# Other transfers of the wk words, products ahead of the first TensorE work, another order of the first tasks, and branch hints

## The chip, the cores and the metric

One NeuronCore of a Trainium2 chip runs the kernel. The metric is the device time of one execution in microseconds, the median of several runs. TensorE (PE; PEld is its weight load), VectorE (DVE), ScalarE (ACT), GpSimd (POOL) and SyncE (SP, which issues the DMAs here) each work through a list of their own and wait for each other by semaphores.

## The reference

Gated linear attention over 768 steps for 4 x 8 heads of width 48, then a channel mix over 3072 rows of 384:

```python
f = 1.0 / (1.0 + np.exp(-f_logit))
for t in range(S):
    state = f[:, :, t, :, None] * state + np.einsum('bhd,bhe->bhde', k[:, :, t], v[:, :, t])
    y[:, :, t] = np.einsum('bhd,bhde->bhe', q[:, :, t], state)
...
xk = mu_k * x + (1.0 - mu_k) * x_prev
xr = mu_r * x + (1.0 - mu_r) * x_prev
k = np.maximum(xk @ w_k, 0.0)
v = k * k @ w_v
r = 1.0 / (1.0 + np.exp(-(xr @ w_r)))
return (r * v).astype(np.float32)
```

## The kernel before

The attention runs in 24 chunks of 128 steps (index i), the mix in 8 units of 384 rows (index u); three chunks fill one unit. Everything is written as small named tasks, and the table ORDER sets, token by token, in which order the tasks' instructions stand; each engine gets its own instructions in that order. A suffix such as `:V` picks the engine where a task has several. HOMES names the buffer of each pool that a task takes.

The tasks of a chunk, in the order in which they depend on each other: loads `f`, `qk`, `v`; `sf` (DVE, a clamp of the logits); for the first six chunks `zT` (PE transposes), `ez` and `ln` (ACT), `b` (PE, running sums by a triangular matrix), `rb` and `e` (ACT); `q` (DVE) and `kr` (DVE or POOL) scale q and k; `TR` (PE transposes) and `kt` (copy) turn k; `SP` (PE, scores and state sums); `m` (mask), `zb` and `T` (DVE, the new state), `za` (POOL); `YA`, then `w`, then `YB` (PE, the chunk's output), `y` (ACT, the output into x and a stage). Then `sp` (16-row DMAs that spread the stage over x), `d`, `xm`, `xh`, `xl` (the mixed input, split in a high and a low part).

The tasks of a unit: `F` (8 groups of 9 products with wk), `r`, `h`, `kk`, `l` (the squares, split), `R` (3 groups of 9 with wr), `lg` and `sg` (the sigmoid), `W` (6 groups of 12 with wv), `o` and `out`. F0.0 is the first of these groups.

The weights arrive as 8-byte words. A piece p of wk, wr or wv passes `S`, `T`, `X` (DVE), `H` (ACT or DVE, the high part) and `L` (POOL or DVE, the low part). F0.f waits for wkL of its own 128 columns. wk comes in eight transfers of 384 KB, each with 128 of its 1024 columns, so that one row of a transfer is 1 KB; four land before the first unit and four later.

At the end, `lo` (DVE) reduces two checks to a column, `lot` (PE) transposes it, `lom` (DVE) makes a flag of it, and `strong` loads the flag into a register of every engine. After the token `?` stands a branch: where the flag is set, a slow general form runs in place of what was computed. With these inputs it is skipped. Only o7.2 and its transfer stand behind it.

`+n` puts n products of constants on PE (`fill`), which nobody reads.

Of the kernel before, what the change touches and what calls it, by code (L numbers as in the profile page):

```python
# [60 lines left out]
e4 wrH2 y1 qk5 wvX0 wrS3 wk1 wrT3 zb2 TR3 bl4 YA2 wrX3 m2 kr4 w2:V q4 q3 T2 kt3 wrH3 b5 wkL0 rb5 YB2 wrL3 v4 y2 wvS2 wkS3
sp0.0 TR4 SP3 wvT2 wvH0 wkT3 x00 za3:G wrL2 e5 sp0.2 wvL0 wvX2 zb3 YA3 wvH2 m3 sp0.1 kr5 wkS1 w3 kt4 v5 wrH0 YB3 y3 T3 za4:G
wvL2 d0.00 wkT1 SP4 q5 wk5 wkX1 wkX3 xm0.00 wr1 bl5 wkH1 d0.10 zb4 +2 YA4 d0.02 xh0.00 m4 wk4 TR5 w4 T4 wrL0 YB4 d0.01 xm0.02
wkL1 wk6 kt5 xl0.00 xm0.01 za5:G SP5 xm0.10 wk7 xh0.02 wv3 y4 zb5 x01 xh0.01 f2 wv4 m5 xl0.02 YA5 d0.12 d0.11 xl0.01 w5:V wkH3
xm0.12 YB5 wrS1 xh0.10 wkL3 F0.0 xm0.11 xl0.10 F0.1 xh0.11 y5 wrT1 xh0.12 wkS4 wrX1 wkS5 r0.0 wkT4 xl0.11 kk0.0:A wrH1 wkT5
xl0.12 wkX4 r0.1 F0.2 wkX5 wrL1 h0.0 kk0.1:A wkS6 wkT6 l0.0 R0.0 wkH5 wkS7 wkH4 r0.2 wkX6 wkL4 h0.1 wkH6 wkT7 F0.3 wkL6 l0.1:V
kk0.2:A wkX7 wvS3 F0.4 wkH7 wkL5 lg0.0 wvT3 wkL7 h0.2 r0.3 wvX3 kk0.3:A F0.5 l0.2 sp1.1 wvS4 wvH3 r0.4 h0.3 wvL3:V h0.4:G F0.6
kk0.4:A wvT4 wv5 r0.5 f3 l0.3:V wvX4 h0.5 sp1.0 l0.4:V F0.7 r0.6 kk0.6:A R0.1 kk0.5 qk7 sp1.2 r0.7 l0.5:V wvH4:V h0.7:G
kk0.7:A wvS5 qk8 R0.2 lg0.1 wvT5 wvX5 h0.6 qk6 l0.7 l0.6 W0.00 v7 wvL4:V lg0.2 wvH5 sg0 wvL5:V d1.0 W0.01 xm1.00 d1.1 xh1.00:V
xm1.11 W0.10 xm1.01 xl1.00:V sf3 xh1.01:V d1.2 W0.11 xm1.12 sf2 xl1.01 xm1.02 xm1.10 b6 xh1.02 ln6 xl1.02 W0.20 o0.0 o0.1  # L70
W0.21 out0.0 rb6 bl6 b7 c1 ln7 q7 q6 F1.0 rb7 kr6 xh1.10 bl7 kr7 o0.2 n7 v6 n6 out0.2 k7 F1.1 xl1.10 r1.0 v8 b8 kk1.0:A qk9
h1.0 l1.0 F1.2 r1.1 k6 ln8 kk1.1 rb8 TR6 q8 kr8 TR7 kt6 SP6 r1.2:V kt7 xh1.12 kk1.2 bl8:V b9 g8 h1.2 F1.3 zb6:A l1.2 xh1.11 n8
# [951 lines left out]
```

## Time and profile before

| | us |
|---|---|
| median of 3 runs | 337.22 (335.83 to 338.24) |
| the profiled execution, device time | 335.34 |
| its span, first to last instruction | 333.5 |
| PE busy in the span | 318.3 (95%) |
| DVE busy | 257.6 (77%) |

The profile is of one execution. The time is 1.8 us more than the span. [...] In a timeline row, the bracket is the engine's idle time before the instruction and what ended it. A row in which several instructions are merged has its count behind an x.

### The profile page before, as it was taken

How to read it: one execution, taken by the hardware profiler on the slowest of the kernel's cores; microseconds unless marked ns; L12 is line 12 of the kernel's file. 1: busy time of each engine (PE TensorE's matmuls, PEld its weight loads, DVE VectorE, ACT ScalarE, POOL GpSimd, SP SyncE). 2: the span in 40 equal slices, each digit the busy share in tenths (PEclk: the TensorE clock that was granted, in tenths of full speed). 3: DMA queues.
4: the chain of work that ended last, by engine and by line, in shares of the span. 5: the costliest groups of instructions: out<-in, count | busy, mean ns of one | idle time of the engine just before them, and what ended most of it. 6: DMA issues, size and time to landing. Idle time of an engine off the chain costs nothing.

```text
span 333.5 us, 10954 instructions
## 1 busy us (share of the span) xinstructions
PE 318.3 (95%) x4560; PEld 304.5 (91%) x4560; DVE 257.6 (77%) x517; ACT 180.9 (54%) x366; POOL 163.3 (49%) x212
## 2 busy tenths in 40 slices
PE   4896899999999999999999999999999999999994
PEld 4685789999999989999999998999999999999994
DVE  4898899999989988897877776698679817767530
ACT  3795888869376565593549234475247132604510
POOL 2278786377653434114762858317565015326500
PEclk9999699999999999999999999999999999999999
DMA  7987693834436333943315522506024003243001
GB/s 260 366 327 233 175 329 87 317 111 137 175 99 191 108 108 117 303 161 101 105 32 211 210 89 79 183 0 191 11 63 135 28 6 96 93 134 110 2 28 56
DMA packets 21370, 46.41 MB, mean 139 GB/s; under 512 B 3008, under 2 KB 13760, under 8 KB 21312
## 3 DMA queue, kind: packets, MB, share of 16 engines
q1 hardware_dynamic: 21312, 45.63, 41.4%
q8 instruction: 38, 0.62, 0.7%
q14 instruction: 20, 0.16, 0.1%
HBM read 38.54 MB, written 4.72 MB: 130 GB/s over the span
## 4 chain that ended last, share of the span: by engine, by line
PE 87%; DMA 5%; DVE 2%; ACT 2%; SPq 2%; issue 1%; POOL 0%; DVEq 0%; ACTq 0%
PE pm L561 72%; PE py L408 7%; PE pss L371 3%; DMA f<-in_zt 3%; PE pss L391 2%; DMA words_k2l<-in_wk 2%; PE py L349 2%; SPq L693 1%; PE pm L342 1%; POOL wv L707 0%; SPq L457 0%; ACT f L261 0%; PE py L766 0%; DVE qk L287 0%; SPq L232 0%
## 5 line engine op out<-in xcount | busy, mean ns | idle before, releaser
L561 PE MATMUL pm<-xh,wk 128*128 128x384 f32 x384 | 103.8, 341 | 0.9 <-DVE qk L295 0.6
L561 PEld LDWEIGHTS pm<-xh,wk 128*128 128x128 f32 x384 | 69.9, 187 | 2.1 <-DVE qk L295 1.1
L561 PE MATMUL pm<-xl,wk 128*128 128x384 f32 x192 | 64.7, 337 | 0.0
L584 ACT ACTIVATE r<-pm 128x384 f32<-128x384 f32 x46 | 22.4, 492 | 50.1 <-PE pm L561 43.7
L561 PE MATMUL pm<-wv,k2h 128*128 128x384 f32 x192 | 49.2, 338 | 0.0
L553 POOL TENSOR_TENSOR xl<-xm,xh 128x384 fp32r<-128x384 f32 x28 | 29.4, 1058 | 31.0 <-DVE xh L547 19.3
L601 POOL TENSOR_TENSOR k2l<-kk,k2h 128x384 fp32r<-128x384 f32 x32 | 34.1, 1069 | 17.7 <-ACT k2h L589 9.9
L287 POOL TENSOR_TENSOR qk<-qk,rb 128x256 f32<-128x256 f32 x21 | 16.0, 761 | 46.6 <-ACT bl L276 21.8
L561 PE MATMUL pm<-wr,xh 128*128 128x384 f32 x144 | 37.0, 338 | 0.0
L561 PEld LDWEIGHTS pm<-xl,wk 128*128 128x128 f32 x192 | 36.0, 188 | 0.4 <-issue 0.4
L590 POOL TENSOR_TENSOR k2h<-r 128x384 fp32r<-128x384 f32 x27 | 25.8, 958 | 21.2 <-ACT r L584 13.5
L561 PEld LDWEIGHTS pm<-wv,k2h 128*128 128x128 f32 x192 | 34.5, 188 | 0.2
L561 PE MATMUL pm<-wv2h,k2h 128*128 128x384 f32 x96 | 32.7, 341 | 0.0
L561 PE MATMUL pm<-wv2l,k2h 128*128 128x384 f32 x96 | 32.3, 336 | 0.0
L561 PE MATMUL pm<-wv,k2l 128*128 128x384 f32 x96 | 32.3, 336 | 0.0
L561 PE MATMUL pm<-wv2h,k2l 128*128 128x384 f32 x96 | 32.3, 336 | 0.0
L601 DVE TENSOR_TENSOR k2l<-kk,k2h 128x384 fp32r<-128x384 f32 x32 | 22.5, 707 | 8.7 <-ACT k2h L589 4.9
L561 PEld LDWEIGHTS pm<-wr,xh 128*128 128x128 f32 x144 | 25.8, 188 | 0.2
L408 PE MATMUL py<-qk,z 64*64 64x64 f32 x704 | 22.2, 233 | 3.7 <-DVE z L328 2.9
L538 DVE SCALAR_TENSOR_TENSOR xm<-pm,mu_sb,x 128x384 f32<-128x384 f32 x42 | 24.9, 610 | 0.8 <-POOL xl L553 0.5
L561 PE MATMUL pm<-wr,xl 128*128 128x384 f32 x72 | 24.2, 336 | 0.0
L595 POOL TENSOR_TENSOR kk<-r 128x384 f32<-128x384 f32 x14 | 12.5, 891 | 22.1 <-ACT r L584 14.6
(143 smaller groups left out, 702.4 us busy)
## 6 DMA issues: line engine op xcount, KB each, us to landing
qk<-in_qkt SPq DMA_DIRECT2D x24, 512.0 KB, 4.8
words<-in_wv SPq DMA_DIRECT2D x12, 512.0 KB, 4.6
f<-in_zt SPq DMA_DIRECT2D x7, 768.0 KB, 7.3
v<-in_vt SPq DMA_DIRECT2D x24, 192.0 KB, 3.9
out<-o SPq DMA_DIRECT2D x21, 192.0 KB, 2.1
...
```

Source lines behind the costliest of these rows:

```text
L287: e.tensor_tensor(k()[:, ::2], k()[:, ::2], rb()[:, ::2], op=ALU.mult)
L349: nc.tensor.transpose(self.py[:, r, 256 + 64 * j : 320 + 64 * j], k()[HALF[r], j], self.ident[HALF[r], HALF[r]])
L371: nc.tensor.matmul(self.pss[HALF[h], r, 64 * j : 64 * j + 64], k()[HALF[r], j, HALF[h]], q()[HALF[r], j, HALF[h ^ j % 2]], start=True, sto ...
L391: nc.tensor.matmul(self.pss[64 * r : 64 * r + D, h, n : n + D], self.b("ktk", i)[HALF[h], j, r], self.b("v", i)[HALF[h], 2 * j + r], start ...
L408: first[c, h] = nc.tensor.matmul(to, lhs, rhs, start=(c, h) not in first, stop=stop, skip_group_check=True)
L538: pl.add(f"xm{u}.{n}{j}", pr, ("V", 0.62, 0, lambda xm=xm, n=n, j=j: nc.vector.scalar_tensor_tensor(xm(), pm("d", u, j)[:, :UT], self.mu_s ...
L553: e.tensor_tensor(lo(), xm(), hi().bitcast(F32), op=ALU.subtract)
L561: nc.tensor.matmul(ps, lhs(a, j), rhs(bb, j), start=ends[0] and i == 0, stop=ends[1] and i == len(pr) - 1)
L584: pl.add(f"r{u}.{f}", kf, ("A", 0.5, 0, lambda r=r, ps=ps: nc.scalar.activation(r(), ps(), AF.Relu)), ("V", 0.56, 0, lambda r=r, ps=ps: nc ...
L590: ("G", 1.02, 0, lambda r=r, hi=hi: nc.gpsimd.tensor_tensor(hi(), r(), r(), op=ALU.mult)),
L595: ("G", 1.02, 0, lambda r=r, kk=kk: nc.gpsimd.tensor_tensor(kk(), r(), r(), op=ALU.mult)),
L601: e.tensor_tensor(lo(), kk(), hi().bitcast(F32), op=ALU.subtract)
```

## The change

Four things change.

- wk comes in four transfers of 768 KB. Three of them hold 768 columns of one third of wk's rows each (one row of a transfer is 6 KB), the fourth the last 256 columns. One such transfer makes two pieces. F0.0 to F0.2 now each wait for the three pieces wkL0, wkL1 and wkL2, F0.3 to F0.5 for wkL3, wkL4 and wkL5.
- Seven products of a new constant tile `warm` stand at the head of PE's list, and the later fills use the same tile. `warm` is set by DVE's first instruction.
- ORDER and HOMES are new. On PE the tasks of the attention's first six chunks are reordered, with fills of 7, 3, 2, 2 and 4 products where there were 3, 2 and 2; behind F0.0 few PE tasks change places, one of them `lot`.
- A branch hint stands ahead of the load of the flag on every engine, for the branch over the general form.

The diff, cut to its core. Of the two tables one line each stands here:

```diff
-f0.0 qk0 sf0.0 f0.2 cst mu zT0 f0.1 ez0 sf0.2 sf0.1 wr2 v0 wk2 ln0 qk1 wk0 +3 b0 f1 v1 wv1 rb0 zT1 kr0:V ez1 v2 e0 zT2 TR0 qk2
++7 f0.0 cst qk0 v0 v1 f0.1 mu f0.2 wr2 sf0.0 zT0 ez0 qk1 wk2 f1 ln0 +3 b0 sf0.1 rb0 zT1 wk0 wv1 qk2 kr0:V wrS2 ez1 qk3 ln1 v2
...
-    "words": "010101010010100110010",
+    "words": "010100101100101010101",
...
-                   + ([] if alone else [f"wkL{f}"]),
+                   + ([] if alone else [f"wkL{p}" for p in (range(f // KJ * KJ, f // KJ * KJ + KJ) if f < 2 * KJ else (f,))]),
...
+                for h in range(2):
+                    p = (6 if last else i) + (h if last else KJ * h)
...
+                    piece("wk", p, home, view, lambda i=i, last=last: self.wk[:, :, 6 * P :] if last else self.wk[:, i, : 6 * P],
...
+                          i, h == 0, whole, 6 * P)
...
     def fill(self, what):
 
         for _ in range(int(what)):
-            self.nc.tensor.matmul(self.py[:, 0, 256:384], self.low[:, 0], self.low[:, 1], start=False, stop=True,
-                                  skip_group_check=True)
+            to = self.tiles["pm"][3][:, :P] if self.cold else self.py[:, 0, 256:384]
+            self.nc.tensor.matmul(to, self.warm, self.warm, start=self.cold, stop=True, skip_group_check=True)
+        self.cold = False
...
         def load():
+            self.tc.mark_branch_hint_location("rest", "LikelyTaken", engines=mybir.ALL_ENGINES)
             self.strong = nc.values_load(self.flag, min_val=0, max_val=1)
...
+    nc.vector.memset(k.warm, LOW)
...
-    with tc.If(k.strong > 0):
+    with tc.If(k.strong > 0, label="rest"):
```

What the new tables do at three places follows; the numbers behind names are those of buffers.

PE's list at its head, before: `ident,f` is zT, `low` a fill, `tri,f` is b, `ident,qk` is TR, and the rows with pss are SP.

```order
L256 MATMUL pm_93<-ident,f_61 128x128 x4
L766 MATMUL py<-low 128x128 x3
L250 MATMUL pm_94<-tri,f_61 128x128 x4
L256 MATMUL pm_95<-ident,f_61 128x128 x4
L256 MATMUL pm_96<-ident,f_61 128x128 x4
L342 MATMUL pm_93<-ident,qk_64 128x128 x4
L250 MATMUL pm_95<-tri,f_61 128x128 x4
L371 MATMUL pss<-qk_64 64x64 x16
```

And now:

```order
L786 MATMUL pm_97<-warm 128x128 x7
L258 MATMUL pm_97<-ident,f_61 128x128 x4
L786 MATMUL py<-warm 128x128 x3
L252 MATMUL pm_95<-tri,f_61 128x128 x4
L258 MATMUL pm_96<-ident,f_61 128x128 x4
L786 MATMUL py<-warm 128x128 x2
L344 MATMUL pm_97<-ident,qk_64 128x128 x4
L252 MATMUL pm_96<-tri,f_61 128x128 x4
L373 MATMUL pss<-qk_64 64x64 x16
```

Seven products stand ahead of zT0, zT2 has gone from before TR0 to behind SP0, and a fill of two stands ahead of TR0.

DVE's list where the first piece of a late wk transfer is turned, before: L685, L696 and L699 are S, T and X of a piece, L328 is zb3, L383 m3, L334 T3.

```order
L279 TENSOR_TENSOR qk_67<-qk_67,pm_96 128x512
L334 TENSOR_TENSOR sm<-pss,z_75 128x192
L685 TENSOR_SCALAR pm_93<-words_122 128x512
L685 TENSOR_SCALAR pm_96<-words_k2l_132 128x384
L696 SCALAR_TENSOR_TENSOR pm_93<-words_122,pm_93 128x512
L696 SCALAR_TENSOR_TENSOR pm_96<-words_k2l_132,pm_96 128x384
L699 SCALAR_TENSOR_TENSOR words_122<-words_122,pm_93 128x512
L328 TENSOR_TENSOR z_77<-pss,z_76 128x4x48
L383 TENSOR_TENSOR ss_100<-pss,mask 128x512
```

And now (L385 is m3, L330 zb3, L336 T3):

```order
L687 TENSOR_SCALAR pm_95<-words_123 128x512
L385 TENSOR_TENSOR ss_101<-pss,mask 128x512
L699 SCALAR_TENSOR_TENSOR pm_95<-words_123,pm_95 128x512
L330 TENSOR_TENSOR z_78<-pss,z_77 128x4x48
L702 SCALAR_TENSOR_TENSOR words_123<-words_123,pm_95 128x512
L336 TENSOR_TENSOR sm<-pss,z_78 128x192
L687 TENSOR_SCALAR pm_97<-words_k2l_133 128x384
L699 SCALAR_TENSOR_TENSOR pm_97<-words_k2l_133,pm_97 128x384
L702 SCALAR_TENSOR_TENSOR words_k2l_133<-words_k2l_133,pm_97 128x384
```

The first instruction that needs the late wk transfer stood ahead of zb3 and now stands behind it, and behind T3.

PE's list at the end, before, from `lot` (L800) on; 20 more products of W7.10 and W7.11 follow the four below, then `TENSOR_LOAD flag`, then W7.20:

```order
L561 MATMUL pm_94<-wv2h,k2l_958 128x384
L800 MATMUL pm_93<-ident,xm_112 1x128 x2
L561 MATMUL pm_96<-wv_87,k2h_859 128x384
L561 MATMUL pm_96<-wv_88,k2h_859 128x384
L561 MATMUL pm_96<-wv_87,k2l_864 128x384
L561 MATMUL pm_96<-wv_87,k2h_859 128x384
```

And now, `lot` being L820, up to the first products of W7.20:

```order
L563 MATMUL pm_96<-wv2l,k2h_967 128x384
L563 MATMUL pm_96<-wv2h,k2l_970 128x384
L820 MATMUL pm_97<-ident,xm_112 1x128 x2
L1043 BRANCH_PREFETCH_HINT
L832 TENSOR_LOAD flag
L563 MATMUL pm_94<-wv_88,k2h_860 128x384
L563 MATMUL pm_94<-wv_89,k2h_860 128x384
```

Between `lot` and PE's load of the flag stood 24 products; now there is none.

## Rows read from the trace of the kernel before

**Rows 1.** The page's parts 1 and 2: busy time, and slices.

```profile
PE 318.3 (95%) x4560; PEld 304.5 (91%) x4560; DVE 257.6 (77%) x517; ACT 180.9 (54%) x366; POOL 163.3 (49%) x212
...
PEclk9999699999999999999999999999999999999999
```

**Rows 2.** Chain that ended last, in time: start, us, what.

```profile
33.59 1.56 PE py L408 x48
...
39.14 0.84 PE py L408 x48
...
45.06 33.27 PE pm L561 x189
...
320.59 8.39 PE pm L561 x48
```

**Rows 3.** Busy time by stretch: us, PE, PEld, DVE, ACT, POOL, clock, DMA share, GB/s.

```profile
30.00:36.40 6.40, 4.25 (x184) 3.97 (x176) 5.78 (x13) 2.85 (x10) 4.86 (x6) 0.64 0.37 110
36.40:41.71 5.31, 4.67 (x149) 3.85 (x140) 4.35 (x9) 5.10 (x14) 4.25 (x7) 0.79 0.78 232
```

**Rows 4.** DVE's timeline: start, us, engine, line, operation.

```profile
0.88 0.06 DVE L882 MEMSET sure<- 128x1 f32 x1 [0.88 <-PEq L1010]
...
3.62 0.49 DVE L460 TENSOR_SCALAR f<-f,sure 128x512 f32<-128x512 f32 x1 [0.33 <-DMA f<-in_zt]
...
9.10 0.43 DVE L287 TENSOR_TENSOR qk<-qk,rb 128x256 f32<-128x256 f32 x1 [2.10 <-ACT rb L263]
...
29.99 0.56 DVE L685 TENSOR_SCALAR pm<-words_k2l 128x384 int32<-128x384 int32 x1 [1.10 <-DMA words_k2l<-in_wk]
...
36.40 0.62 DVE L533 SCALAR_TENSOR_TENSOR xm<-x,one_mu,pm 128x384 f32<-128x384 f32 x1 [0.62 <-ACT pm L530]
```

**Rows 5.** PE's timeline up to the first product of F0.0.

```profile
4.25 1.09 PE L256 MATMUL pm<-ident,f 128*128 128x128 f32 x4 [4.25 <-DVE f L460]
5.13 1.49 PE L766 MATMUL py<-low 128*128 128x128 f32 x6
6.69 1.74 PE L250 MATMUL pm<-tri,f 128*128 128x128 f32 x8
...
10.63 1.16 PE L250 MATMUL pm<-tri,f 128*128 128x128 f32 x8 [0.17 <-ACT f L261]
...
32.62 0.71 PE L408 MATMUL py<-qk,z 64*64 64x64 f32 x16 [1.88 <-DVE z L328]
...
42.91 0.44 PE L561 MATMUL pm<-xh,wk 128*128 128x384 f32 x1
```

**Rows 6.** POOL's timeline: the last low parts ahead of F0.0.

```profile
40.15 2.05 POOL L553 TENSOR_TENSOR xl<-xm,xh 128x384 fp32r<-128x384 f32 x2 [0.17 <-ACT xh L546]
```

**Rows 7.** DMA issues by line: KB each, median us to landing.

```profile
f<-in_zt SPq DMA_DIRECT2D x7, 768.0 KB, 7.3
...
words_k2h<-in_wk SPq DMA_DIRECT2D x2, 384.0 KB, 7.6
```

**Rows 8.** The flag's tile, its makers and loads (duration min/median/max ns, start us).

```profile
L807 DVE SCALAR_TENSOR_TENSOR flag<-xm x1: 148/148/148, 321.2 to 321.2; 1x1 int32<-1x1 f32 x1
...
L811 PEldq TENSOR_LOAD <-flag x1: 487/487/487, 321.5 to 321.5; - x1
```

**Rows 9.** All engines' timeline from `lot` to o7.2.

```profile
320.21 0.38 PE L800 MATMUL pm<-ident,xm 128*1 128x128 f32 x2
320.32 0.30 PEld L561 LDWEIGHTS pm<-wv,k2h 128*128 128x128 f32 x2
...
329.06 0.56 DVE L655 TENSOR_TENSOR lg<-pm,lg 128x384 f32<-128x384 f32 x1 [3.68 <-PE pm L561]
```

**Rows 10.** Line 899, the branch: each engine's compare, and what follows it.

```profile
L899 SPq EVENT_SEMAPHORE  x8: 17/17/17, 328.4 to 329.0; - x8
...
L899 SPq COMPARE_BRANCH  x1: 45/45/45, 325.8 to 325.8; - x1
L899 DVEq EVENT_SEMAPHORE  x1: 21/21/21, 327.7 to 327.7; - x1
```

More of the change, by code (lines that the diff above doesn't have):

```diff
@@ L61 @@
[L61 to L72, printed above, removed]
@@ new lines @@
+wvH0 onemu wrL0 wrX3 ln5 wvS2 qk5 wrH3 b5 m3 wvT2 kt4 sp0.0 wkL3 wrL3 zb3 +2 YA3 rb5 wvL0 wvX2 sp0.1 T3 e5 w3 YB3 wvH2 SP4
+wkS1 za4:G v5 wkT1 d0.02 wkX1 y3 wvL2 xm0.02 q5 wkH1 wr1 kr5 bl4 zb4 wv4 d0.00 bl5 xm0.00 d0.01 wk3 +4 YA4 wkL1 TR5 m4 wv3 w4
+f2 xh0.00 T4 d0.10 xm0.01 xl0.00 YB4 xm0.10 qk6 kt5 xh0.02 SP5 za5:G y4 wrS1 xl0.02 xh0.01 zb5 d0.11 m5 xl0.01 YA5 wrT1 w5 YB5
+d0.12 xm0.11 xh0.10 wrX1 xl0.10 xh0.11 F0.0 wkS4 y5 xm0.12 wrH1 xl0.11 xh0.12 sp1.0 wkT4 wkS5 wkX4 F0.1 r0.0 sp1.1 wrL1 h0.0
@@ new lines @@
+W6.20 xm7.12 xm7.11 xh7.10 o6.1 W6.21 xh7.11 xh7.01:V cm12 out6.1 xl7.01:V F7.0 o6.2 cm2 c13 F7.1 F7.2 r7.0:V kk7.0:G xl7.10
+r7.1:V c10 h7.0 out6.2 F7.3 h7.1 l7.0 cm13 r7.2 kk7.1:A kk7.2 h7.2 r7.3:V l7.1 xh7.12 F7.4 h7.3:G kk7.3 xl7.11:V xl7.12 F7.5
+cm10 R7.0 r7.5:V F7.6 l7.2 r7.4 lg7.0:V kk7.4 l7.3:V h7.4 l7.4 r7.6:V kk7.5:A h7.5:G h7.6:G lo F7.7 r7.7:V h7.7:G R7.1 W7.00
+l7.5:V kk7.6 lg7.1 R7.2 l7.6 kk7.7:G l7.7 lg7.2:V W7.01 W7.10 W7.11 sg7 lot lom strong o7.0 out6.0 o7.1 out7.1 W7.20 W7.21
@@ L667, in add_words, with piece @@
         nc = self.nc
-        def piece(name, p, home, view, load, shape, hi, lo, first):
+        def piece(name, p, home, view, load, shape, hi, lo, src, first=True, whole=None, total=0, begins=True):
             place = WORDS[name][0] + WORDS[name][1] * p
@@ L690, in piece @@
             kept = [home] if home else []
-            tu = {"takes" if first else "uses": kept}
-            free = [f"wkL{j}" for j in range(4, 8)] if name == "wv" and p >= 3 and not clamp else []
-            pl.add(f"{name}{p}", place - 0.4, ("Q", n * P * 8 / 370e3, 1, lambda: nc.sync.dma_start(view(), load())), **tu)
+            free = [f"wkL{j}" for j in (2, 5, 6, 7)] if name == "wv" and p >= 3 and not clamp else []
+            if first:
+                pl.add(f"{name}{src}", place - 0.4, ("Q", (total or n) * P * 8 / 370e3, 1, lambda: nc.sync.dma_start(
+                    (whole or view)(), load())), **{"takes" if begins else "uses": kept})
             dve = us(0.00104, 0.15)
-            pl.add(f"{name}S{p}", place, ("V", dve, 0, shift), after=[f"{name}{p}"], takes=[t_key], uses=kept)
+            pl.add(f"{name}S{p}", place, ("V", dve, 0, shift), after=[f"{name}{src}"], takes=[t_key], uses=kept)
             pl.add(f"{name}T{p}", place, ("V", dve, 0, lambda: nc.vector.scalar_tensor_tensor(
@@ L847, in rwkv_kernel @@
     k.tri = cp.tile([P, P], F32, name="tri")
+    k.warm = cp.tile([P, P], F32, name="warm")
     k.sure = cp.tile([P, 1], F32, name="sure")
```

148 lines of the change are left out of this document (81 added, 67 removed).

## The prediction

> **What bounds the kernel now.** I read the page's busy times first: PE is busy for 318.3 of 333.5 us, and from the sixth slice on the granted clock stands at full [rows 1]. The chain of waits then tells where PE is the bound: from 45.06 us on it runs through 189 wk, wr and wv products in 33.27 us without a gap, 0.176 us each, and at the end through 48 products in 8.39 us, 0.175 each [rows 2]. From F0.0 at 42.91 us [rows 5] to the last product, then, time is PE work, which the change leaves as it is (72 F, 27 R and 72 W products a unit). Only two stretches can give or take time: the head, up to F0.0, and the places where a new order leaves PE with nothing to do.
>
> In the head no single engine is full. What moves it is a chain through all of them, and DVE's idle time shows its stops: 2.10 us for the first `rb`, 1.10 us at 29.99 for a late wk transfer, 0.62 us at 36.40 for ACT [rows 4]. By stretches DVE stands still for 6.40 - 5.78 = 0.62 us and then for 5.31 - 4.35 = 0.96 us [rows 3]. [...] The same kind of YB group costs 1.56 us at 33.59 and 0.84 us at 39.14 [rows 2].
>
> **The products at the head.** The clock column says full from the first slice on [rows 1], but the durations say otherwise: `b0` takes 1.74 us at 6.69, the same eight records 1.16 us at 10.63 [rows 5]. [...] The seven `warm` products need a memset that is DVE's first instruction, where another stands now at 0.88 us [rows 4], so they can start at about 1.1. Three such products are six records and take 1.49 us at the low clock [rows 5], so seven take some 3.2 to 3.5 us and end at about 4.3 to 4.6. zT0 starts at 4.25, when its logits have come and been clamped: the products cost 0.05 to 0.35 us there, of which the faster zT0 behind them (up to half of 1.09 us) gives some back. If the clock rises as long after PE's first product as it does now, it is up by about 5 us, and `b0`, which waits for ACT and not for the fill, saves 1.74 - 1.16 = 0.58 us. The extra memset is hidden: DVE waits 0.33 us for the first logits behind its memsets [rows 4]. I take 0.6 us for this part; the ends are 0 (the clock rises no sooner) and 1.1 (zT0 at the full clock too).
>
> **The four transfers.** Until F0.0 three transfers of 768 KB must have landed instead of four of 384 KB, 2.3 MB instead of 1.5. Yet a transfer of 384 KB with rows of 1 KB has 7.6 us from issue to landing in the median, and one of 768 KB with rows of 6 KB (f, 1536 floats a partition) 7.3 [rows 7]. So I cost the doubled size at nothing; the other end, by size alone, is twice 7.6 us from issue to landing, and DVE would then wait for the first two. The pieces stay 384 columns wide, and so do the DVE, ACT and POOL instructions for them: 12 DVE steps for wk, 9 for wr and 9 for wv stand ahead of zb5 in either order.
>
> **The order.** What moves the most is the late transfer: the wait of 1.10 us stood ahead of zb3 and of all that follows it. Now its first reader stands behind T3, some ten DVE instructions later, and this wait should go. What is late next is POOL and PE: F0.0 needs the third `xl`, which POOL ended at 42.20 [rows 6], and YB5, which PE ended just before 42.91. DVE's idle time behind the first `rb` that can go is 1.10 + 0.62 + 0.96 = 2.68 us [rows 3, 4]. Not all of it will: zb0 is now on DVE, ahead of the first wk piece, and waits there for SP0, and everything behind it on DVE waits with it; the kt, za and xl of the last chunks stand behind three wv pieces on POOL as before. I take half, 1.34 us. The ends are 2.68 and a loss of 1.0: two more fill products stand ahead of YA3, and two more ahead of YA4 on PE's list, at 0.5 us each if the clock is low there.
>
> Behind F0.0 the order of PE's list is all but the old one. F0.0 to F0.2 need three pieces of wk, but these are done before the third `xl`; F0.3 needs wkL5 only four groups later, 36 products or 6.3 us. I put this at nothing, with 0.5 us of PE waiting as its price if POOL is late.
>
> **The end.** Here the change takes time. `lot` stood ahead of 24 products, and now PE's load of the flag stands right behind it. PE's list is worked in order, so W7.20 can't start before that load has ended, which waits for DVE's `lom`, which waits for `lot`. The chain is in the trace: `lot` ends on PE as the next weights load at 320.32 [rows 9], DVE writes the flag at 321.2 + 0.15, and PE's load runs from 321.5 for 0.49 us, to 321.99 [rows 8]. All of that lay beside 24 products (4.2 us). Now W7.20's weights load at the earliest where it ends: 321.99 - 320.32 = 1.67 us in which PE does nothing, on the path that sets the end. The ends are 1.2 (part of the flag's steps is quicker) and 2.0 (the hint ahead of the load takes time too).
>
> [...]
>
> **The hints.** SP's compare stands at 325.8, and what follows it on SP runs at 328.4 to 329.0; DVE is past its branch at 327.7 [rows 10]. So the branch takes SP 2.6 us. But DVE's last instruction waits for the last product until 329.06 [rows 9], and both engines are past the branch before that. Taking it away gives nothing; the cover is 1.3 us on DVE. [...]
>
> **The sum**, on the profiled execution of 335.34 us: -0.6 (clock) - 1.34 (waits in the head) + 1.67 (end) = -0.27, so 335.1. That execution is 1.9 us below the median of the three, so the same difference from 337.22 gives 336.9.
>
> **The rivals.**
> - All of DVE's idle time goes and the clock holds through the 30s: -0.6 - 2.68 + 1.67 = -1.6, 335.6 us. For it: PE has more fills there, so fewer gaps. Against: `zb0` on DVE. Chance 0.17.
> - The end costs nothing, since products behind the load get ahead of it: -1.9, 335.3. For it: nothing in the rows, which show only a load that was ready before PE came to it. Against: a list in order. Chance 0.06.
> - The clock falls again in the thirties, as it does now, and the new fills run at half speed in front of YA3 and YA4: -0.6 + 1.0 + 1.67 = +2.1, 339.3. For it: the sequence SP, zb, YA with PE waiting on DVE is unchanged in kind, and a gap of 1.88 us was there when the clock fell. Against: the late transfer no longer makes that gap. It decides if PE's wait ahead of YA3 stays. Chance 0.16.
> - [...] Chance 0.05.
> - The change doesn't do what it says in the head: the three big transfers land later than the small ones, DVE waits for them, and the head gains nothing: -0 + 1.67, 338.9. Against: the rows on f's transfers. Chance 0.08.
> - My forecast, 336.9: 0.48.
>
> **How the numbers follow.** A measurement of this kernel tells little under 1% (3.4 us) from no change: three runs of it lie 2.4 us apart. Below 333.8 no case of mine reaches by itself; I leave 0.08 for gains in the head that I don't see. Above 340.6 lies the clock at the end, and something of the third case: 0.08. The range goes from 334.3, the second case with half of the runs' spread, to 339.3, the third.
>
> **What would show it.** In the profile after: records of `warm` from about 1.1 us and `b0` in 1.2 us; no DVE wait for a wk transfer around 30 us; the first F0.0 product at about 41.0 instead of 42.91; 48 products of PE's end no longer in one piece, but a gap of 1.6 to 1.8 us between `lot` and W7.20, ended by PE's load. I am wrong if F0.0 starts later than 42.5 or before 39.5, or if no such gap is there.

## The result, and the profile after

The changed kernel takes 342.27 us in the median of 6 runs (340.12 to 346.08) against 336.75 before, a ratio of 1.0144 with the interval 1.0095 to 1.0193: slower by 1.4%, where 336.9 was forecast. Medians and ranges hold every execution; ratios and their intervals leave out single ones that ran some per cent longer at a lower clock, so they aren't the quotients of the medians. Timed once more beside other kernels it took 344.34 (1.0192, 1.0147 to 1.0237). So medians from different series can lie 2 us apart for the same kernel, and below the ratio to the kernel before, timed in each series, is what tells kernels of different series apart. Its profiled execution took 342.51 us with a span of 340.8, 7.3 us over the span before.

The page's parts 1 and 2 after, for [rows 1]:

```profile
PE 322.2 (95%) x4582; PEld 307.4 (90%) x4582; DVE 262.6 (77%) x544; ACT 177.7 (52%) x354; POOL 156.1 (46%) x198
...
PEclk9999979999999999999999999999999999999998
```

The 22 more records of PE are the eleven more clock products (the fills and the seven at the head), two records each. The low figure of the clock (the granted TensorE clock, in tenths of the full one) has moved from the fifth slice (6 before), ahead of F0.0, to the sixth (7), behind it. PE's timeline after, for [rows 5], at the head and around F0.0 (in brackets what the engine waited for):

```profile
1.13 3.35 PE L786 MATMUL pm<-warm 128*128 128x128 f32 x14 [1.13 <-DVE sure L905]
4.33 1.08 PE L258 MATMUL pm<-ident,f 128*128 128x128 f32 x4
5.21 1.49 PE L786 MATMUL py<-warm 128*128 128x128 f32 x6
6.77 1.40 PE L252 MATMUL pm<-tri,f 128*128 128x128 f32 x8
...
41.41 0.46 PE L410 MATMUL py<-qk,z 64*64 64x64 f32 x16 [0.74 <-DVE z L330]
42.22 0.46 PE L410 MATMUL py<-qk,z 64*64 64x64 f32 x16 [0.34 <-ACT done L430]
42.50 0.50 PE L410 MATMUL py<-ss,v 64*48 64x64 f32 x19
45.20 0.67 PE L410 MATMUL py<-ss,v 64*48 64x64 f32 x13 [2.20 <-issue]
45.79 0.69 PE L563 MATMUL pm<-xh,wk 128*128 128x384 f32 x1
```

`warm` is there and `b0` takes 1.40 us instead of 1.74. The rest of the head's gain isn't: YB5 begins at 42.22 (before: 42.07), and in its midst PE stands still for 2.20 us, waiting for no engine ("issue"). F0.0 comes at 45.79 instead of 42.91. In the kernel before, YB5 and the place of such a gap, behind F0.0's ninth product:

```profile
42.07 0.46 PE L408 MATMUL py<-qk,z 64*64 64x64 f32 x16 [0.34 <-DVE done L429]
...
45.06 0.34 PE L561 MATMUL pm<-xh,wk 128*128 128x384 f32 x1 [0.30 <-issue]
```

Busy time by stretch (columns as in [rows 3]) shows what DVE won and lost ahead of YB5, and what follows the stall; the first fence is the kernel before up to its YB5, the second the changed one:

```profile
0.00:42.07 42.07, 32.35 (x799) 27.49 (x799) 33.08 (x76) 29.44 (x68) 24.84 (x43) 0.92 0.80 273
```

```profile
0.00:42.22 42.22, 33.82 (x821) 28.72 (x821) 34.24 (x77) 29.92 (x70) 24.79 (x43) 1.00 0.80 286
44.80:48.21 3.41, 3.02 (x21) 2.87 (x21) 1.16 (x3) 1.42 (x4) 1.45 (x3) 0.51 1.00 367
```

DVE's idle time ahead of YB5 falls from 42.07 - 33.08 = 8.99 to 7.98 us, but its work there grows by 34.24 - 33.08 = 1.16. Of that, 0.91 are two more steps of a wr piece, `wrS1` (40.45, ahead of zb5) and `wrT1` (41.78); in the old order both stand behind YB5. DVE is full there, 11.90 of the 12 us from 24 to 36. That its work sets YB5's time is not shown, though: the chain of waits that the profile follows comes to YB5 by another way, through ACT's list and a transfer of the outputs into x:

```profile
35.10 3.13 DMA x<-stage
```

Then the granted clock falls to half for 3.41 us (0.51 in the second fence's last row), in the last products of YB5 and the first of F0.0. In the chain of waits after, for [rows 2], stall and slow products stand one behind the other; a piece of 189 products costs 34.42 us instead of 33.27 (the old piece begins nine products later, behind the gap of 0.30 us):

```profile
43.00 2.20 issue
45.86 34.42 PE pm L563 x189
...
331.64 4.44 PE pm L563 x24
```

In the second unit the changed kernel has a wait that the one before hasn't (the timeline at QT8, chunk 8's products with `ident`):

```profile
87.97 0.27 PE L351 MATMUL py<-ident,qk 64*128 64x64 f32 x2 [0.92 <-DVE qk L293]
88.46 0.40 PE L351 MATMUL py<-ident,qk 64*128 64x64 f32 x6 [0.21 <-DVE qk L297]
```

And the end, for [rows 8, 9]: `lot`, the flag on DVE, W7.20 behind PE's load of it, the last o7.2 on DVE, and out7.2's issue on SP:

```profile
329.95 0.38 PE L820 MATMUL pm<-ident,xm 128*1 128x128 f32 x2
...
330.91 0.15 DVE L827 SCALAR_TENSOR_TENSOR flag<-xm 1x1 int32<-1x1 f32 x1
...
331.64 0.59 PE L563 MATMUL pm<-wv,k2h 128*128 128x384 f32 x2 [1.31 <-DVE flag L827]
...
336.16 0.56 DVE L657 TENSOR_TENSOR lg<-pm,lg 128x384 f32<-128x384 f32 x1 [3.41 <-PE pm L563]
...
337.50 0.34 SPq L661 DMA_DIRECT2D out<-lg  x1
```

PE's load of the flag starts at 331.1 and takes 491 ns. out7.2 goes out 0.78 us after o7.2 has ended (336.72); before it was 0.02.

All kernels here have the same 3714 PE products from F0.0 to the end, so their records can be counted back from the last one. This table, worked out so from the traces, says where the time went: the start of F0.0, then the time between the starts of the products with the numbers given (from F0.0 on), and last the time from the last product's start to the span's end.

| trace | F0.0 | 0-72 | 72-300 | 300-700 | 700-1000 | 1000-1500 | 1500-2000 | 2000-2500 | 2500-3600 | 3600-last | tail |
|---|---|---|---|---|---|---|---|---|---|---|---|
| before | 42.91 | 13.24 | 27.97 | 13.17 | 22.31 | 33.64 | 24.87 | 33.51 | 97.44 | 19.57 | 4.90 |
| after | 45.79 | 13.89 | 29.27 | 13.16 | 23.19 | 34.15 | 24.87 | 32.57 | 97.71 | 21.13 | 5.05 |
| e3 | 47.91 | 15.16 | 29.27 | 13.16 | 23.17 | 34.17 | 24.87 | 32.57 | 97.68 | 19.59 | 4.01 |
| e7 | 45.71 | 12.71 | 27.88 | 13.16 | 22.31 | 34.12 | 24.87 | 32.57 | 97.67 | 19.59 | 4.01 |
| e10 | 42.47 | 14.67 | 27.99 | 13.17 | 22.31 | 33.58 | 24.87 | 33.48 | 97.44 | 19.57 | 4.03 |
| e12 | 42.76 | 13.15 | 28.12 | 13.16 | 22.31 | 33.57 | 24.87 | 32.57 | 97.81 | 19.59 | 4.19 |
| e18 | 47.62 | 15.35 | 27.93 | 13.16 | 23.61 | 34.11 | 24.87 | 32.57 | 97.63 | 19.59 | 4.03 |

So of the 7.3 us, 2.9 stand ahead of F0.0, 0.65 behind it up to product 72 (0.95 in slow products, less the old gap of 0.30 us, which lies here), 1.3 in the second unit, 0.9 and 0.5 from 700 to 1500, 1.56 at the end; 0.94 are won between 2000 and 2500. From product 1000 to the last one, the rows with the same order agree within 0.2 us; the head is what varies most.

### The profile page after: what moved, and what is told of

Same layout as the page of the kernel before. It is cut to its first block, busy times and chain, and to the rows that moved or that the text cites. A ratio compares the mean times of both kernels' runs of the same rounds, so it can differ in the third digit from the quotient of the medians.

```text
span 340.8 us, 10966 instructions
## 1 busy us (share of the span) xinstructions
PE 322.2 (95%) x4582; PEld 307.4 (90%) x4582; DVE 262.6 (77%) x544; ACT 177.7 (52%) x354; POOL 156.1 (46%) x198
## 4 chain that ended last, share of the span: by engine, by line
PE 76%; DVE 7%; DMA 6%; ACT 3%; SPq 3%; issue 3%; POOL 0%; POOLq 0%; DVEq 0%; ACTq 0%
PE pm L563 65%; PE py L410 6%; DMA qk<-in_qkt 4%; PE pss L373 2%; PE py L351 2%; DMA x<-stage 2%; PE pss L393 2%; DMA f<-in_zt 1%; DVE pm L270 1%; SPq L510 1%; SPq L508 1%; DVE xm L540 1%; DVE qk L281 1%; DVE ss L385 1%; DVE pm L302 1%
## 5 line engine op out<-in xcount | busy, mean ns | idle before, releaser
L555 POOL TENSOR_TENSOR xl<-xm,xh 128x384 fp32r<-128x384 f32 x30 | 34.2, 1146 | 44.6 <-DVE xh L549 20.0
L603 POOL TENSOR_TENSOR k2l<-kk,k2h 128x384 fp32r<-128x384 f32 x40 | 41.3, 1035 | 21.3 <-ACT kk L596 11.9
L592 POOL TENSOR_TENSOR k2h<-r 128x384 fp32r<-128x384 f32 x29 | 25.1, 872 | 41.5 <-ACT r L586 22.3
L586 ACT ACTIVATE r<-pm 128x384 f32<-128x384 f32 x39 | 19.0, 491 | 38.8 <-PE pm L563 36.6
L289 POOL TENSOR_TENSOR qk<-qk,rb 128x256 f32<-128x256 f32 x12 | 9.6, 798 | 35.7 <-ACT rb L265 9.4
L591 ACT ACTIVATE k2h<-r 128x384 fp32r<-128x384 f32 x35 | 18.0, 519 | 10.8 <-DVE r L587 10.5
L596 ACT ACTIVATE kk<-r 128x384 f32<-128x384 f32 x35 | 18.0, 521 | 10.2 <-DVE k2l L603 5.3
```

Source lines behind the costliest of these rows:

```text
L289: e.tensor_tensor(k()[:, ::2], k()[:, ::2], rb()[:, ::2], op=ALU.mult)
L555: e.tensor_tensor(lo(), xm(), hi().bitcast(F32), op=ALU.subtract)
L586: pl.add(f"r{u}.{f}", kf, ("A", 0.5, 0, lambda r=r, ps=ps: nc.scalar.activation(r(), ps(), AF.Relu)), ("V", 0.56, 0, lambda r=r, ps=ps: nc ...
L591: pl.add(f"h{u}.{f}", kf, ("A", 0.53, 0, lambda r=r, hi=hi: nc.scalar.activation(hi(), r(), AF.Square)), ("G", 1.02, 0, lambda r=r, hi=hi: ...
L592: ("G", 1.02, 0, lambda r=r, hi=hi: nc.gpsimd.tensor_tensor(hi(), r(), r(), op=ALU.mult)),
L596: ("A", 0.53, 0, lambda r=r, kk=kk: nc.scalar.activation(kk(), r(), AF.Square)),
```

## The experiments

### What PE's stall is

Counted in the traces, the stall of 2.20 us stands behind PE's 855th matmul record, and so does the gap of 0.30 us in the kernel before, which is there between F0.0's ninth product and F0.1's first. 22 records lie between the two places, as many as the new clock products have. A packet of q8, a DMA queue that the page lists as `instruction` (38 packets, 0.62 MB in either trace), moves just then. I took the stall for a wait of PE for its instructions, a fetch; no record of a trace names it so. Two kernels move the place.

**e1_seven_fills**

```diff
- +7 f0.0 cst ... wk3 +4 YA4
+ f0.0 cst ... wk3 YA4
```

> The changed kernel with only seven clock products ahead of F0.0, as the kernel before has (the seven at the head of PE's list and the four ahead of YA4 are dropped). Theory A (an instruction fetch): PE's stall of 2.20 us at 43.00 stands at a fixed place of PE's instruction list, behind its 855th matmul record in both kernels; 22 records fewer ahead of it put it behind nine products of F0.0 again, where before lost 0.30 us, since the slow products cover the fetch. So no stall over 0.5 us, no 1.2 GHz behind it: -2.2 + 0.3 - 1.15, and +0.3 for the head's clock, 339.5 us against 342.3 (338.8 to 341). Theory B (the load on the DMA queues, from the four big transfers): a stall of about 2 us stays inside YB5, 342 to 343.

341.11 us (340.33 to 341.54; 1.0147, 1.0124 to 1.017): by its ratio no faster than the changed kernel (1.0144), though with the narrowest spread of all. The place moved as theory A said, behind F0.0's ninth product, and no lower clock follows it (1.00 from 40 to 50 us). But the gap didn't shrink to 0.5 us. PE's timeline:

```profile
45.63 0.34 PE L563 MATMUL pm<-xh,wk 128*128 128x384 f32 x1
47.39 0.45 PE L563 MATMUL pm<-xh,wk 128*128 128x384 f32 x1 [1.42 <-DVE pm L699]
```

**e2_before_eleven**

```diff
- zb3 YA3 ... xl0.02 YA5
+ zb3 +8 YA3 ... xl0.02 +3 YA5
```

> The kernel before with eleven more clock products where PE waits anyway: eight ahead of YA3 (it waits 1.88 us there) and three ahead of YA5 (0.64 us). Its transfers stay small. Theory A (an instruction fetch at a fixed place of the list): 22 records more put the place behind record 35 of YB5's last 48, and a stall of 1.5 to 2.4 us appears there, with 1.2 GHz behind it: +1.9 + 1.1, less up to 1 us that a clock held up through the thirties gives back, 338.5 to 340 against 336.8. Theory B (the big transfers): no stall over 0.5 us there, 336 to 337.

340.72 us (337.94 to 346.95; 1.012, 1.0076 to 1.0165). Eleven clock products alone, with the old transfers and the old order, cost 1.2%, or 4.0 us: more than even theory A forecast. The stall of YB5 is there, and a lower clock behind it (7 tenths in the slice from 42.3 us); F0.0 comes at 45.61, much as in the changed kernel. The timeline of e2:

```profile
43.42 0.51 PE L408 MATMUL py<-ss,v 64*48 64x64 f32 x20
45.25 0.43 PE L408 MATMUL py<-ss,v 64*48 64x64 f32 x12 [1.32 <-issue]
45.61 0.45 PE L561 MATMUL pm<-xh,wk 128*128 128x384 f32 x1
```

But the stall in YB5, 1.32 us, isn't all of it. F0.0 is 2.70 us later than in the kernel before, since YB5 itself begins 1.06 us later, at 43.13; behind F0.0, 1.07 us more go up to product 72, 0.65 from 700 to 1000 and 0.62 at the tail.

The packet of q8, the instruction queue, ties the stalls together. In each of the traces with a gap at record 855 (856 in e2) PE goes on 1.2 to 1.5 us after that packet has ended (before: packet from 42.76 for 0.99, next product 45.06; after: 42.51 for 1.38, 45.20; e1: 45.11 for 0.98, 47.39). So I take the wait in e1 that the profile puts down to DVE for the fetch too. Where the packet ended over 1.5 us before PE came (e7: 45.25 against 47.20, and e16: 44.76 against 47.91), there is no gap. The gap's length varies at either place: 0.30, 0.33, 0.66 and 1.78 us behind the ninth product of F0.0 with the old order (before, e12, e15, e10), 1.42 and 1.17 there with the new one (e1, e8), and 1.16 to 4.07 inside YB5 (e2 and the traces with the new head and all 18 clock products). A gap of the same kind stands at record 473 (0.51 us of "issue" in the kernel before, at 29.70, 1.30 us after a packet from 27.42 for 0.97), 382 records earlier, some three times 127. A packet has 16 KB (0.62 MB in 38), and there are 4560 matmul records with as many loads, some 36 times 127: from these numbers I estimate a block, what one packet brings, at 127 matmul records with their weight loads. In the traces with a gap, 0.3 to 4.1 us of PE's time go to it.

The next boundary ahead of 855 is then record 728, by the estimate, and the two kernels differ in how fast PE gets from the one to the other: from record 728 to 855 the old head takes 39.70 to 44.42 = 4.7 us, since nine F0.0 products of some 0.17 us are among them; the new head 39.32 to 42.78 = 3.5, all short ones. The fetch takes 5.4 and 5.9 us in these two traces, if it is counted from PE's passing of record 728 to its going on. Its packet starts 3.1 and 3.2 us after that passing; that it is asked for there, no run shows.

### What makes the fetch long

**e5_late_two**

```diff
- w4 f2 xh0.00 ... xm0.10 qk6 kt5 ... F0.1 r0.0
+ w4 xh0.00 ... xm0.10 kt5 ... F0.1 qk6 f2 r0.0
```

> The changed kernel with two issues moved on SP's list from ahead of YA5 to behind F0.1: f2 (768 KB, wanted by the second unit's last chunks) and qk6 (512 KB, wanted at the second unit). Theory A2: the stall at PE's 855th matmul record is an instruction fetch that is asked for when PE crosses the boundary 128 records earlier, and its length is set by the bytes that stand in the DMA queues then; from crossing to the fetch's first packet it was 3.1 us in the kernel before, 3.2, 4.4 and 5.5 in three traces of changed kernels. With 1.28 MB fewer queued, the fetch starts within 1 to 2 us, the stall falls from 2.2 to 4.2 us to under 1 us, and the clock doesn't fall behind it: 338.5 to 340 us against 342.3. Rival: the length has nothing to do with these two; the stall stays at 2 to 4 us, 342 to 343.

345.53 us (1.0252, 1.0202 to 1.0302), and the stall is as it was, 2.25 us. From record 728 to the packet's start it took 3.3 us. The theory in this form falls.

**e9_late_four**

```diff
- zb4 wv4 d0.00 ... m4 wv3 w4 f2 xh0.00 ... xm0.10 qk6 kt5 ... F0.1 r0.0
+ zb4 d0.00 ... m4 w4 xh0.00 ... xm0.10 kt5 ... F0.1 wv3 wv4 qk6 f2 r0.0
```

> The changed kernel with four issues moved from ahead of YA5 to behind F0.1: wv3 and wv4 (512 KB each), qk6 (512 KB) and f2 (768 KB), so that between 37 and 42 us only wr1 (288 KB) and wk3 (768 KB) go out. With f2 and qk6 alone moved, the fetch still started 3.3 us after PE crossed the boundary. Theory A3: the fetch's delay is the time in which the queues drain what was issued before it; with 1.06 MB (some 2.7 us at the 400 GB/s that the head shows) instead of 2.1 to 3.4 MB, issued by 39 us, it starts within 1 us of the crossing and the stall at the 855th matmul record is under 0.5 us; F0.0 follows YB5's middle without a gap and the ninth product behind it comes 2.5 to 3.5 us sooner. Rival: the delay is not the transfers', the stall stays at 2 us or more.

344.17 us (1.0223, 1.0178 to 1.0269). With four transfers out of the way the stall is at its shortest for this head, and the fetch takes 40.78 to 45.62 = 4.8 us, the least of all with a gap; but the stall is not gone, and the time isn't better:

```profile
43.97 0.49 PE L407 MATMUL py<-ss,v 64*48 64x64 f32 x19
45.62 0.67 PE L407 MATMUL py<-ss,v 64*48 64x64 f32 x13 [1.16 <-issue]
```

Nor were the queues empty. The last two columns of these stretches are the DMA share and GB/s:

```profile
40.00:42.00 2.00, 1.56 (x96) 1.50 (x96) 1.30 (x3) 2.00 (x7) 1.13 (x2) 1.00 0.94 309
42.00:44.00 2.00, 0.91 (x49) 0.68 (x42) 1.92 (x5) 2.00 (x7) 2.00 (x3) 1.00 0.61 219
44.00:46.00 2.00, 0.84 (x44) 0.70 (x33) 2.00 (x6) 0.94 (x3) 1.66 (x3) 0.85 0.03 12
```

The packet started at 43.19, when the transfers were nearly done. So e9 missed the half microsecond of stall that theory A3 forecast, but it doesn't test a fetch without load: load on the queues may lengthen the fetch, and no trace with a gap here has the queues idle ahead of the packet. What sets its length between 4.8 and 7.8 us stays open.

### Transfers or order of the head

**e6_qk2_first**

```diff
- qk1 wk2 f1 ... zT1 wk0 wv1 qk2 kr0:V
+ qk1 qk2 wk2 f1 ... zT1 wk0 wv1 kr0:V
```

> The changed kernel with qk2's transfer (512 KB) issued ahead of the first big wk transfer (wk2) instead of behind the second one (wk0) and a wv transfer. It lands 12.21 us after its issue in the changed kernel, POOL waits 4.71 us for it and PE 1.14 us for POOL. Theory: the two 768 KB transfers ahead of qk2 hold up the chunk chain; without that PE's wait of 1.14 us and 0.5 of the next go, and F0.0 comes 1 to 1.5 us sooner if DVE, which is full from 24 to 36 us, isn't what bounds the head. Rival: DVE bounds it, and DVE then waits for wk2 or wk0 instead: no change, 342 to 343.

344.59 us (1.0233, 1.0181 to 1.0285), YB5 at 43.88 and F0.0 at 47.80: no gain.

**e11_halves** (`wk0b`, `wk1b`, `wk2b` issue the second 384 columns)

```diff
- self.wk[:, i, : 6 * P]
+ self.wk[:, i, c]
- qk2 ... wk1 ... qk5
+ wk0b wv1 qk2 ... wk1 wk1b ... qk5 wk2b
```

> The changed kernel with three of the four wk transfers sent as two halves of 384 KB (384 columns each, the same bytes in all); the second half of wk2 goes out behind qk5 at about 31 us, those of wk0 and wk1 right behind their first halves. So 384 KB fewer stand ahead of qk2. Theory (the big transfers hold up the chunk chain): qk2 lands 1 us sooner, PE's wait of 1.14 us for it goes, and YB5 is reached 0.5 to 1 us sooner, 341 to 341.8. Rival (DVE, full from 24 to 36 us with 1.2 us more work ahead of YB5 than in the kernel before, bounds the head): no change, 342 to 343.5.

343.87 us (1.0192, 1.0148 to 1.0235), YB5 at 42.56, the stall 2.1 us: no change.

**e13_small_transfers** (the functions of the kernel before, without the hints, with `warm` and its memset; the new order, the wk pieces renumbered so that it stands)

```diff
- zT0 ez0 qk1 wk2 f1 ... zT1 wk0 wv1 qk2
+ zT0 ez0 qk1 wk0 f1 ... zT1 wk1 wk2 wv1 qk2
```

> The changed kernel's order and clock products with the eight wk transfers of 384 KB of the kernel before (and without the hints). If the big transfers cost the head its time, YB5 is reached at 41.5 to 42 us and the stall falls to what the old transfers show (0.3 to 2): 339 to 340. If the order of the head does it, YB5 comes at 42.5 to 44 us with a stall of 2 to 4 us as in the changed kernel: 342 to 344.5.

345.29 us (1.0246, 1.0198 to 1.0294). With the small transfers back, the changed order is no faster. By YB5's start alone, 41.95 as in the old head, the expectation would have blamed the big transfers; but the changed kernel has 42.22 and e4, with the big ones, 42.02, and the stall takes F0.0 to 45.23 all the same:

```profile
41.95 0.46 PE L407 MATMUL py<-qk,z 64*64 64x64 f32 x16 [0.34 <-ACT done L427]
42.23 0.49 PE L407 MATMUL py<-ss,v 64*48 64x64 f32 x19
44.87 0.43 PE L407 MATMUL py<-ss,v 64*48 64x64 f32 x13 [2.14 <-issue]
45.23 0.44 PE L560 MATMUL pm<-xh,wk 128*128 128x384 f32 x1
```

**e14_old_head_big** (to be compared with e12, below)

```diff
- wk2 ... wk0 ... wk3 ... wk1 ... wk5 ... wk4 ... wk6 ... wk7
+ wk2 ... wk0 ... wk1 ... wk3
- F0.3 wkL6 ... wkL5
+ wkL5 F0.3 wkL6
```

> The last kernel of the runs before (old head, new order from the third unit on, lot early, hints: 335.1 us, F0.0 at 42.76) with the four transfers of 768 KB in place of the eight. If the big transfers cost the head its time: F0.0 1 to 2.5 us later, 336.5 to 338. If not: 335 to 335.7.

336.03 us (0.9976, 0.9942 to 1.0009), where e12 has 0.9962 (0.9935 to 0.9989): the big transfers alone cost nothing that can be told. It is the order and the clock products that cost the head, and each does so without the other. Counted to the start of product 72, the traces take 55.9 to 57.4 us with the old order and its seven clock products (before, e10, e12, e15), 59.9 with eleven more (e2), 58.4 to 59.6 with the new order and seven (e1, e7, e8), and 59.5 to 63.1 with the new order and all 18 (after, e3 to e6, e9, e11, e13, e18).

### Behind F0.0

**e4_second_unit**

```diff
- W0.11 xl1.01:V xh1.10 sf2 o0.0 F1.0 sf3 b6 xh1.12 o0.1 W0.20 out0.1 b7 ... F2.0
+ W0.11 xm1.12 sf2 xl1.01 xm1.02 xm1.10 b6 xh1.02 ln6 xl1.02 W0.20 o0.0 o0.1 W0.21 out0.0 ... F1.0 ... F2.0
```

> The changed kernel with the order of the kernel before from the end of the first unit's F products (W0.00) to F2.0, and the new order ahead of it and behind it. If PE's 1.7 us of idle time between 87.9 and 88.7 us (QT8 waiting for DVE's k8) come from the new order of the second unit, with F1.0 ahead of W0.20, they go: 340.4 to 341. If they come from the state in which the first unit leaves the engines (later by 2.9 us at F0.0), they stay: 342 to 342.6.

342.49 us (1.0192, 1.0154 to 1.0229), but the stretch from 72 to 300 falls from 29.27 to 27.93, the time before, and the waits at QT8 are gone. In its trace F0.0 came at 47.46, which hides the gain. And 0.93 us of "issue" stand at product 876, matmul record 1744: seven blocks of 127 behind record 855, 1.45 us after a packet of the instruction queue, so by the place and the packet the same kind of stall.

**e3_lot_early**

```diff
- W7.01 W7.10 W7.11 sg7 lot lom strong
+ W7.01 sg7 lot W7.10 lom W7.11 strong
```

> The changed kernel with the order of the end as before (lot ahead of W7.10, lom ahead of W7.11). If the wait of 1.31 us ahead of W7.20 is PE's load of the flag behind lot, it goes: -1.3. If out7.2 stands behind SP's branch (issued 337.50, 1.3 us behind o7.2's end, where before needed 0.02), that goes too: up to another -0.8 to -1.3. So 341.0 by the first alone, 339.7 to 340.2 with both; 342.3 if the wait only moves to another place.

342.22 us (1.0176, 1.0143 to 1.0208). Between 3600 and the last product 21.13 become 19.59, and the tail 5.05 becomes 4.01: 2.6 us as forecast; its time doesn't show them, with F0.0 at 47.91. PE has no gap behind `lot` now:

```profile
329.14 0.38 PE L820 MATMUL pm<-ident,xm 128*1 128x128 f32 x2
...
329.27 0.60 PE L563 MATMUL pm<-wv,k2h 128*128 128x384 f32 x2
```

**e17_changed_again** (the changed kernel, nothing edited)

> The changed kernel as it is, as the control for the one-part runs. If its head varies from run to run by the length of the instruction fetch, its median lies at 343 to 344.5 and the runs spread over 4 us or more, so that the medians of the one-part kernels (342.2, 342.5) do lie 1 to 2 us below it. If 342.3 holds within 0.5 us, the two gains seen in the traces are lost elsewhere.

344.34 us (340.53 to 346.65; 1.0192, 1.0147 to 1.0237): the control does lie 2 us higher beside the others, and e3's and e4's ratios, 1.0176 and 1.0192, can't be told from it.

**e18_second_and_lot** (the edits of e4 and e3)

> The changed kernel with the second unit in the old order up to F2.0 and lot ahead of W7.10, its head and its 18 clock products kept. If the terms add: 1.36 + 1.54 + 0.8 to 1 less than the control in the same run, 3.7 to 3.9 us; and what is left over the kernel before, 2.5 to 5 us, lies in F0.0's start. If they trade: 0 to 1.5 us less.

341.63 us (1.0121, 1.0078 to 1.0165), 2.7 us under the control of the same run, of the 3.9 that the traces show for the two (1.34 in the second unit, 1.54 and 1.02 at the end). They add up for the most part. What is left over the kernel before lies in the head (F0.0 at 47.62, and slow products up to product 72) and, with 1.3 us, from 700 to 1000, where 0.99 us of "issue" stand at record 1744 again.

**e7_together** (the edits of e1, e3, e4 and e5)

> The changed kernel with all that the runs pointed to: seven clock products ahead of F0.0 (as in the first run: 341.1, with no 1.2 GHz left), f2 and qk6 behind F0.1, the second unit in the old order up to F2.0 (1.36 us less between the 200th and the 300th product behind F0.0), and lot ahead of W7.10 (1.54 us of PE and 0.8 us at the tail less). If each term holds: 341.1 - 1.4 (stall) - 1.4 - 2.4 = 335.9, level with the kernel before. If the stall stays: 337.3. If the terms trade against each other (PE's waits only move), 339 to 340.

336.93 us in 12 runs (1.0007, 0.9976 to 1.0037): level with the kernel before, 1 us over the forecast. F0.0 still comes at 45.71, but without a stall behind it.

### The hints

**e8_together_no_hint**

```diff
- self.tc.mark_branch_hint_location("rest", "LikelyTaken", engines=mybir.ALL_ENGINES)
- with tc.If(k.strong > 0, label="rest"):
+ with tc.If(k.strong > 0):
```

> The last kernel without the branch hints (the flag's load and the branch as in the kernel before). If the hints do nothing, the same time within 0.5 us, and SP stands as long behind its compare. If they bring the taken code in ahead, this one is up to 1 us slower, with out7.2 issued later behind the end of o7.2 on DVE. If the hint instruction itself costs time, up to 0.5 us faster.

337.76 us (1.0035, 1.0008 to 1.0062), 0.8 us over e7 in the same run, whose interval (0.9976 to 1.0037) overlaps with this one.

**e10_before_hints** (the two lines of e8, the other way round, in the kernel before)

> The kernel before with the branch hints alone. In traces with hints and lot ahead of W7.10 the span ends 4.01 and 4.02 us after the last product's start, without hints 4.89, 5.18 and 5.51, since SP's instruction fetch then runs beside out7.2's transfer. Theory: -0.9 at the tail, 335.8 us against 336.7. My prediction's view: nothing (336.7 within 0.3).

335.33 us against 336.58 in the same run (0.9964, 0.9932 to 0.9995): about 1.2 us faster, with 0.2 to 2.3 by the interval; my prediction's view falls. From out7.2's issue to its last packet the traces with hints and `lot` ahead of W7.10 have 1.5 us (e3, e7, e10, e12), those without hints 2.0, 2.3, 2.4 and 2.9 (e13, before, e8, e2); in these four a packet of the instruction queue starts 0.2 to 0.5 us after that issue (in before one of q8, at 330.12), in the others it has ended by then (e15 and e16, below, also have 1.5). That it is SP's fetch, as I expected, no trace shows. The 2.6 us of SP's branch in my prediction aren't what the hint takes away: from SP's compare to what follows it are 2.7 to 2.8 us in e3, e7, e10 and e12, where before needed 2.7. PE's branch is what is shorter, 1.0 to 1.5 us in these four, against 3.8 in before, e2 and e8. And the gain isn't sure: in e15 and e16, with hints and an early `lot` too, out7.2 goes out 1.41 and 1.30 us behind o7.2, and the tail is 5.38 and 5.31 us.

### The best of both, and the clock products

**e12_before_then_new** (the kernel before with e10's hints; from W2.21 on, what is left in the new order, with e3's edit)

```diff
- W2.21 rb16 k15 xh3.11 QT15 v15 xl3.02 YA13 kr16 ...
+ W2.21 rb16 k15 xh3.11 QT15 v15 c4 out2.1 YA13 b17 ...
```

> The kernel before up to W2.21 (its head, its small transfers, its order), then the new order, with lot ahead of W7.10, and the branch hints. The new order was 0.94 us shorter between the 2000th and the 2500th product behind F0.0, 0.2 us longer in each of the next two stretches, and the hints took 0.9 us from the tail: 336.7 - 0.94 + 0.3 - 0.9 = 335.2 us. If the 0.94 us came from where the instruction fetch falls in the list and not from the order, 335.8.

335.06 us (0.9962, 0.9935 to 0.9989), faster than both kernels, but no different from e10, the hints alone, by their intervals. In the trace the 0.94 us between 2000 and 2500 are the order's: they are won with the old instruction count too.

**e15_seven_at_head** (e12 with the changed `fill`, the `warm` tile and its memset)

```diff
- f0.0 qk0 ... wk0 +3 b0 f1 ... +2 TR1 ... +2 YA4
+ +7 f0.0 qk0 ... wk0 b0 f1 ... TR1 ... YA4
```

> The kernel with the old head (335.1 us) with its seven clock products moved to the head of PE's list, on a tile whose memset is DVE's first instruction (so the place of the instruction fetch stays). My prediction's term: the clock is up sooner, b0 takes 1.16 to 1.4 us instead of 1.74, -0.3 to -0.6: 334.6. Rival: without the products ahead of b0, TR1 and YA4 the clock comes up later or falls in the thirties, +0.5 to +2: 335.6 to 337.

335.71 us (0.9948, 0.9916 to 0.9979), no different from e12 by their intervals. `b0` takes 2.08 us, as in e12: seven products that end at 4.5 us, with no more ahead of `b0`, don't make it shorter. In e3 and e13, with the three behind them, it takes 1.16. The clock column has 1.00 there in any case (e15 and before, 0 to 12 us), so the durations alone tell of the clock at the head.

```profile
1.13 3.36 PE L766 MATMUL pm<-warm 128*128 128x128 f32 x14 [1.13 <-DVE sure L885]
4.31 1.09 PE L255 MATMUL pm<-ident,f 128*128 128x128 f32 x4
6.75 2.08 PE L249 MATMUL pm<-tri,f 128*128 128x128 f32 x8 [1.35 <-ACT f L260]
```

**e16_three_fills**

```diff
- +2 TR1 ... +2 YA4
+ TR1 ... YA4
```

> The kernel with the old head (335.1 us) without the four clock products ahead of TR1 and YA4: PE's 855th matmul record is then the 18th of F0.0 and F0.1's products instead of the tenth, so that 1.4 us more of slow products cover the fetch. Theory (a fetch at a fixed place): the stall there is 0, -0.3 to -0.7 us, if the clock holds; 334.5. Rival (the fetch waits for more than the products cover): no change, 335.1; with the clock lower through the thirties up to +1.

336.1 us (0.9983, 0.9947 to 1.0019). The gap at record 855 is gone (0.17 us from one product to the next), as a fetch at a fixed place wants it, but the clock is at half (0.50) from 32.22 to 42.46, and F0.0 comes at 45.02 instead of 42.76. The rival's second half, the lower clock, was right.

```profile
32.22:42.46 10.24, 8.57 (x280) 7.67 (x272) 7.08 (x15) 6.86 (x19) 7.56 (x10) 0.50 0.54 160
```

## Why the prediction was wrong

It said -0.6 - 1.34 + 1.67 = -0.27. Measured in the two traces, in the same order: the head gave nothing, and stall and slow products took 3.5; the end took 1.56; and 2.0 came from the stretches that I had put at nothing. F0.0 at 45.79 is past the 42.5 that I had named as the sign of being wrong.

- **The clock, -0.6.** The sign was right: `warm` runs from 1.13, and `b0` takes 1.40 us after and 1.16 in other traces of the same list, where the old head has 1.74 to 2.08 (before, e10, e12). It needs the three fills ahead of `b0` as well (e15: 2.08). None of it is left at YB5. That the clock is the cause, no run shows: its column has 1.00 there.
- **The order of the head, -1.34.** This step failed. I took half of DVE's idle time as won. It did fall, by 1.0 us, and the wait around 30 us is gone, but DVE's work ahead of YB5 is 1.16 us more. My count of "9 for wr" ahead of zb5 "in either order" was wrong: in the new order they are ten, and eleven ahead of YB5, 0.91 us of the 1.16. YB5 stays where it was (42.22) or comes later (42.0 to 43.9 in the other new heads with all 18 clock products, 43.3 to 44.9 in those with seven, 41.6 to 42.1 in three old ones). No run takes these steps out, so whether they, ACT's list or the transfer into x hold YB5 back stays open.
- **Between YB5 and F0.0.** This step failed too, and it is the larger part: no term of mine stood here. The clock products were priced at their own time, 0.5 us for two. What the eleven more cost besides goes, as I read it, with the place of an instruction fetch: 2.20 us of stall instead of 0.30 in these two traces, and 3.41 us of half clock (0.51) behind it, 0.95 us of slow products up to product 72. e2 shows this cost without the other changes, at 4.0 us in all. The gap of 0.30 us of "issue" at 45.06 was in the trace before, and I took the chain from there on as dense.
- **The four transfers, 0.** Held: e13 isn't faster without them, e14 not slower with them by more than its interval.
- **Behind F0.0, 0 with 0.5 as the price.** Wrong by 2.0: +1.3 in the second unit, shown by e4 and e18; +0.9 from 700 to 1000, where PE waits for DVE at two places (ahead of product 894 for `xm`, of 930 for `o`) that cost nothing in e1 and e7, which have seven clock products. Why they cost something with 18 stays open. In e8, which has seven too, the same stretch loses 0.71 us of "issue" at record 1744, 1.33 us after a packet. +0.5, -0.9 and +0.3 later go with the order (e7, e12).
- **The end, +1.67.** Right, with 1.56: W7.20 starts at 331.64, where PE's load of the flag ends (331.1 + 0.49). The clock didn't fall there (1.00 from 329.95 to 336.08). Not seen: out7.2 0.78 us behind o7.2, since SP's branch now ends later than DVE (what follows it on SP runs from 336.5 to 337.4).
- **The hints, 0.** In the changed kernel they bring nothing to see (tail 5.05 against 4.90), but for another reason than the one I gave: with an early `lot` they are worth about 1 us (e10; e8 points the same way), and in the traces with hints and a late `lot` PE's branch takes 3.6 to 4.8 us, as long as without them.
- **The rivals.** The clock fell in neither place that I named, not at the end and not in the thirties (1.00 up to 42.22, where the kernel before has 0.50 from 32 to 38); it fell behind the stall. The 1.2 GHz in the forecasts of e1, e2 and e7 is a term that no run shows: the traces give a share of the full clock, 0.51 behind the stall in the changed kernel and 1.00 in e1 from 40 to 50 us. None of the rivals had the fetch. The one whose head gains nothing, 338.9, had the head's missing gain right and its reason, late transfers, wrong.
